# Moving a row norm from GpSimd to ScalarE, with GpSimd left to form its scale and bias

## The chip, the cores and the metric

The kernel runs on one core of one Trainium2 chip. The metric is the time of one execution in device microseconds (us); lower is better. The engines of the core run unsynchronized and meet by semaphores: TensorE (PE, its weight loads PEld), VectorE (DVE), ScalarE (ACT), GpSimd (POOL) and SyncE (SP), which here issues most of the DMAs.

## The reference, cut to what matters

```python
xn = _layernorm(A_q)                    # rows of 448: (x - mean) / sqrt(var + 1e-5)
k_shift = causal depthwise conv of A_k with 4 taps (A_shift_k)
kv = k_shift * A_v
y  = long causal convolution of kv with A_ssm_k (FFT, length 4096) + kv * A_ssm_D
h  = xn @ B_w1 + B_b1                   # 448 -> 1792
out = A_q + xn * y + mish(h) @ B_w2     # 1792 -> 448
```

There are 2048 rows of 448 numbers, all float32. The change is about how `xn` is formed for the dense part (`h`).

## The kernel before, in words

**Two strands, one TensorE.** The dense part (MLP) runs over 8 chunks of 256 rows; each chunk is two tiles `jj` of 128 rows. Within a chunk 7 pairs `p` of 128 hidden columns are worked one after the other. Between them stand, by hand-written slot numbers, the steps of the long convolution: first transforms of the filter and of `kv` (`f1_mm`, `f1_fold`, `f1_out`, slots up to 63), then eight octants of products (`h2_mm`, `v2_mm`, `prod`, `i1_mm`), then the inverse transform and the gate (`i2_mm`, `gate`). The program order on every engine is the order in which the Python code issues; nothing reorders it.

**A pair.** Pair number i has two slots. Slot 2i: `g1_mm(i)`, 22 matmuls into a PSUM tile `pg` (L447), in float32r with high and low halves. Slot 2i+1: `mish(i)`, where ScalarE reads `pg` into `a` (L455, two instructions), then casts `a` to its high half `ach` (L73), and VectorE forms the low half `acl` (L74); and `g2_mm(i-2)`, 12 matmuls that use `ach` and `acl` (L472 to L474). The PSUM tiles `pg` are a ring of two, shared by `g1_mm` and by the transposes of `xn`: `g1_mm(i+2)` waits until `mish(i)` has read its tile. The tiles `pc` of the convolution are another ring of two.

**The norm.** `ln_stats(c)` puts six small steps for chunk c into a list `drip`; `dv()` takes one from it after each VectorE instruction of other work, so that they are spread out. The first five are VectorE's: `stats` of both tiles (L379), `aggr` of both (L382: mean and variance into `mv`), `eps` (L385: variance plus 1e-5 into `ve`). The sixth issues `power` (L388, GpSimd: `ve` to the power -0.5 into `rstd`), `norm` for both tiles (L392: subtract the mean, multiply by `rstd`) and `tail` (L396: a copy of the last 64 columns behind the row). `norm` and `tail` are on GpSimd for chunks 1 to 6, and on VectorE for chunks 0 and 7.

**What uses it.** `ln_T(c, jj)` transposes `xn` on TensorE (L407), ScalarE casts the result to the high half `XH` (L419), and VectorE forms the low half `XL` (L417). For tile 0 this stands in front of `mish` of the last pair but one of the chunk before, for tile 1 in front of `g1_mm` of the last pair.

**Other work on the same queues.** Chunk 0 also splits weights: ScalarE casts `w2h` (L73) and `w1h` (L338), VectorE forms `w2l` (L74) and `w1l` (L343, L345). For the convolution ScalarE copies `st` (L130), `hs` (L209), `vs` (L218) and `qe` (L249) out of `pc`, and issues the stores of `st` and `qe` on its own DMA queue (L139, L250); VectorE folds `st` (L131, L133), works the taps (L153 to L165) and the products (L231).

Of the kernel before, what the change touches and what calls it, by code (L numbers as in the profile page):

```python
# [7 lines left out]
F32 = mybir.dt.float32  # L8
F32R = mybir.dt.float32r
AF = mybir.ActivationFunctionType  # L10
ALU = mybir.AluOpType
# [3 lines left out]
S, D, F = 2048, 448, 1792  # L15
NJ = 16
# [3 lines left out]
NCHUNK = S // CH  # L20
# [16 lines left out]
def tile_kernel(ctx: ExitStack, tc, q, k, v, sk, hT, sD, w1, b1, w2, c_f1, c_g, c_gi, c_i2, out):  # L37
    nc = tc.nc
    V = nc.vector

    def pool(name, bufs=1, stack=ctx, **kw):
        return stack.enter_context(tc.tile_pool(name=name, bufs=bufs, **kw))

    cp = pool("consts")
# [14 lines left out]
    f1id = cp.tile([128, 2, 128], F32, name="f1id")  # L59
    f1, ident = f1id[:, 0], f1id[:, 1]  # L60
    mhalf = cp.tile([128, 2], F32, name="mhalf")
    b1t = cp.tile([128, NF], F32, name="b1t")
    mv = cp.tile([128, NJ, 2], F32, name="mv")
    rstd = cp.tile([128, NJ], F32, name="rstd")
# [190 lines left out]
    EE, QA, Q = {}, {}, {}  # L255
# [115 lines left out]
    def ln_parts(c):  # L371
        st = mp.tile([128, 2, 6], F32, name="bst", bufs=2)
        ve = mp.tile([128, 2], F32, name="ve", bufs=2)
        xn = mp.tile([128, 2, D + 64], F32, name="xn", tag="xn", bufs=1)
        XN[c] = xn
        eng = nc.gpsimd if 0 < c < NCHUNK - 1 else V

        def stats(jj):
            V.bn_stats(st[:, jj], Q[c][:, jj])  # L379

        def aggr(jj):
            V.bn_aggr(mv[:, 2 * c + jj], st[:, jj])  # L382

        def eps(a, b):
            V.tensor_scalar(ve[:, a:b], mv[:, 2 * c + a:2 * c + b, 1], EPS, None, op0=ALU.add)  # L385

        def power(a, b):
            nc.gpsimd.tensor_tensor(rstd[:, 2 * c + a:2 * c + b], ve[:, a:b], mhalf[:, a:b], op=ALU.pow)  # L388

        def norm(jj):  # L390
            j = 2 * c + jj
            eng.tensor_scalar(xn[:, jj, :D], Q[c][:, jj], mv[:, j, 0:1], rstd[:, j:j + 1],  # L392
                              op0=ALU.subtract, op1=ALU.mult)

        def tail(a, b):
            eng.tensor_copy(xn[:, a:b, D:], xn[:, a:b, D - 64:D])  # L396

        return stats, aggr, eps, power, norm, tail

    def ln_stats(c):  # L400
        stats, aggr, eps, power, norm, tail = ln_parts(c)
        drip.extend([lambda: stats(0), lambda: stats(1), lambda: aggr(0), lambda: aggr(1), lambda: eps(0, 2),
                     lambda: [f(*a) for f, *a in ((power, 0, 2), (norm, 0), (norm, 1), (tail, 0, 2))]])
# [169 lines left out]
            at(t + 2 + m, gate_out, c)  # L573

    V.memset(mhalf, -0.5)
    one = cp.tile([128, NJ], F32, name="one")
    V.memset(one, 1.0)
    ve0 = cp.tile([128, 2], F32, name="ve0")
# [12 lines left out]
    nc.sync.dma_start(b1t, b1)  # L591
    h_load(2)
    stats, aggr, eps, power, norm, tail = ln_parts(0)
    for jj in range(2):
        stats(jj)
# [20 lines left out]
    for s in range(nslots):  # L616
        j = s // 2 - G2_LAG - 1
# [70 lines left out]
```

## Time and profile before

| | |
|---|---|
| time, three runs | 382.29, 382.82, 383.46 us; median 382.82 |
| span of the profiled execution | 382.4 us; the page gives no other time for that execution, and the median of the runs is 0.4 us above it |
| TensorE busy | 368.1 us (96%) |
| VectorE busy | 277.9 us (73%) |
| ScalarE busy | 158.8 us (42%) |
| GpSimd busy | 50.5 us (13%) |
| mean granted TensorE clock | 0.983 |

The busy shares are means over stages that differ: VectorE is above 90% in the stage with the taps and around 50% later. In a timeline row the columns are start, duration, engine, line, operation, written tile<-read tiles, size, count; what stands in brackets is the idle time of the engine before the row and what ended it.

### The profile page before, as it was taken

The page shows a single profiled execution, that of the slowest core. Times are in us where ns is not written, and L with a number is a line of the kernel's source. Part 1 is how long each engine was busy: PE and PEld are TensorE (multiplying, and loading weights), DVE is VectorE, ACT ScalarE, POOL GpSimd, SP SyncE. Part 2 cuts the span into 40 slices and gives each one's busy share as a digit, 9 for nine tenths or more (in the row PEclk, how much of TensorE's full clock was granted, in tenths as well). Part 3 has the DMA queues.
Part 4 walks back from the last instruction along what each step waited for, and adds up shares of the span by engine and source line. Part 5 has one row for each costly group of instructions (what it writes and reads, how often), then busy time and mean ns, then how long its engine had stood idle before and what let it go on. Part 6 is the DMA issues. An engine that isn't in the chain of part 4 may idle for free.

```text
span 382.4 us, 7472 instructions
## 1 busy us (share of the span) xinstructions
PE 368.1 (96%) x3126; PEld 295.4 (77%) x3126; DVE 277.9 (73%) x369; ACT 158.8 (42%) x265; POOL 50.5 (13%) x47
## 2 busy tenths in 40 slices
PE   5999999999999999999999999999999999999984
PEld 1888888978888988988876776667666798768954
DVE  2799858999999998997434745843954724989393
ACT  2587543344233433433443755653755334122310
POOL 2006000700042003200023000240000040220000
PEclk8599999999999999999999999999999999999998
DMA  7799986839588427604885687967570759999566
GB/s 266 288 269 339 363 317 173 250 68 300 126 289 213 117 51 249 192 4 96 255 265 175 207 268 245 289 225 241 199 265 2 243 155 233 239 228 254 194 185 248
DMA packets 32851, 82.11 MB, mean 215 GB/s; under 512 B 2993, under 2 KB 18226, under 8 KB 32818
## 3 DMA queue, kind: packets, MB, share of 16 engines
q1 hardware_dynamic: 22498, 52.72, 43.0%
q10 hardware_dynamic: 9200, 22.50, 19.9%
q0 software_dynamic: 1120, 6.42, 7.1%
q8 instruction: 24, 0.39, 0.4%
q14 instruction: 9, 0.07, 0.1%
HBM read 53.19 MB, written 28.44 MB: 213 GB/s over the span
## 4 chain that ended last, share of the span: by engine, by line
PE 60%; DMA 19%; DVE 13%; ACT 3%; issue 3%; POOL 1%; ACTq 0%; SPq 0%; DVEq 0%
PE pg L447 25%; PE pg L472 7%; PE pc L198 7%; PE pg L474 6%; PE pg L473 6%; DMA e<-E 6%; DMA out_dram<-q 5%; PE pc L124 4%; PE pc L241 3%; DMA a<-ACC 3%; PE pg L407 2%; DVE x L162 2%; DMA kr<-in_k_dram 2%; DMA f1id<-in_c_f_dram 1%; DMA Dkv<-st 1%
## 5 line engine op out<-in xcount | busy, mean ns | idle before, releaser
L455 ACT ACTIVATE a<-pg,b1t 128x256 f32<-128x256 f32 x112 | 47.1, 473 | 122.8 <-PE pg L447 104.8
L447 PE MATMUL pg<-XH,w1h 128*128 128x256 f32 x448 | 92.2, 288 | 1.6 <-DVE XL L417 0.9
L447 PEld LDWEIGHTS pg<-XH,w1h 128*128 128x128 f32 x448 | 70.8, 191 | 18.9 <-issue 15.0
L472 PE MATMUL pg<-w2h,ach 128*128 128x448 f32 x224 | 83.2, 371 | 0.2 <-DVE qt L479 0.2
L474 PE MATMUL pg<-w2h,acl 128*128 128x448 f32 x224 | 81.4, 363 | 0.0
L473 PE MATMUL pg<-w2l,ach 128*128 128x448 f32 x224 | 81.3, 363 | 0.0
L74 DVE TENSOR_TENSOR acl<-a,ach 128x512 fp32r<-128x512 f32 x56 | 38.4, 687 | 48.6 <-ACT ach L73 48.4
L447 PE MATMUL pg<-XL,w1h 128*128 128x256 f32 x448 | 70.4, 279 | 0.0
L447 PEld LDWEIGHTS pg<-XL,w1h 128*128 128x128 f32 x448 | 60.3, 190 | 0.0
L447 PE MATMUL pg<-XH,w1l 128*128 128x256 f32 x336 | 57.4, 280 | 0.0
L472 PEld LDWEIGHTS pg<-w2h,ach 128*128 128x128 f32 x224 | 42.0, 187 | 12.7 <-issue 10.4
L447 PEld LDWEIGHTS pg<-XH,w1l 128*128 128x128 f32 x336 | 47.5, 191 | 0.0
L473 PEld LDWEIGHTS pg<-w2l,ach 128*128 128x128 f32 x224 | 42.1, 188 | 2.5 <-DVE w2l L74 0.2
L474 PEld LDWEIGHTS pg<-w2h,acl 128*128 128x128 f32 x224 | 42.1, 188 | 2.5
L388 POOL TENSOR_TENSOR rstd<-ve,mhalf 128x2 f32<-128x2 f32 (+1 forms) x9 | 7.7, 859 | 265.7 <-DVE ve L385 265.7
L73 ACT CAST ach<-a 128x512 fp32r<-128x512 f32 x56 | 34.7, 620 | 1.8
L392 POOL TENSOR_SCALAR xn<-qt,mv,rstd 128x448 f32<-128x448 f32 x12 | 28.4, 2371 | 0.6
L162 DVE TENSOR_TENSOR x<-x 128x896 f32<-128x896 f32 x24 | 27.0, 1123 | 0.8
L419 ACT CAST XH<-pg 128x512 fp32r<-128x512 f32 x16 | 9.4, 588 | 38.3 <-PE pg L407 38.2
L417 DVE TENSOR_TENSOR XL<-pg,XH 128x512 fp32r<-128x512 f32 x16 | 11.0, 688 | 14.4 <-ACT XH L419 14.1
L130 ACT COPY st<-pc 128x896 f32<-128x896 f32 x16 | 14.5, 909 | 15.6 <-PE pc L124 13.3
L124 PE MATMUL pc<-x,f1id 32*64 32x448 f32 x256 | 17.3, 585 | 3.2 <-DMA f1id<-in_c_f_dram 3.2
(62 smaller groups left out, 394.4 us busy)
## 6 DMA issues: line engine op xcount, KB each, us to landing
Dh<-st ACTq DMA_DIRECT2D x16, 448.0 KB, 5.5
Dkv<-st ACTq DMA_DIRECT2D x16, 448.0 KB, 5.2
ah<-Dh SPq DMA_DIRECT2D x8, 896.0 KB, 5.5
av<-Dkv SPq DMA_DIRECT2D x8, 896.0 KB, 4.8
E<-qe ACTq DMA_DIRECT2D x8, 896.0 KB, 4.1
e<-E POOLq DMA_DIRECT2D x14, 448.0 KB, 14.6
kr<-in_k_dram SPq DMA_DIRECT2D x10, 448.0 KB, 7.1
x<-in_hT_dram SPq DMA_DIRECT2D x8, 448.0 KB, 6.5
```

What stands on the lines that cost most here:

```text
L73: nc.scalar.copy(h, raw)
L74: V.tensor_sub(l, raw, h)
L124: nc.tensor.matmul(ps[h][64 * jj:64 * jj + 64, b, :D], f1[rg:rg + 32, 0:64], x[rg:rg + 32, jj], start=True, stop=True, tile_position=(rg, ...
L130: nc.scalar.copy(st[:, 1], o)
L162: V.tensor_add(KV[g], KV[g], o)
L198: nc.tensor.matmul(p[32 * t:32 * t + 32, r, :D], g[rs, t, c], a[rs, t], start=True, stop=True, tile_position=(64 * r, 32 * t))
L392: eng.tensor_scalar(xn[:, jj, :D], Q[c][:, jj], mv[:, j, 0:1], rstd[:, j:j + 1], op0=ALU.subtract, op1=ALU.mult)
L447: nc.tensor.matmul(ps[:, n], l, r, start=n_ == 0, stop=n_ == len(mm) - 1)
L455: nc.scalar.activation(a[:, n], ps[:, n], AF.Mish, bias=b1t[:, 2 * p + n:2 * p + n + 1])
L472: nc.tensor.matmul(ps, ah[:, n, cs], w2h[:, f], start=f == 0, stop=False)
L473: nc.tensor.matmul(ps, ah[:, n, cs], w2l[:, f], start=False, stop=False)
L474: nc.tensor.matmul(ps, al[:, n, cs], w2h[:, f], start=False, stop=f == NF - 1)
```

## The change

For chunks 1 to 7 `xn` is written by one ScalarE instruction per tile, as `rstd * x + shift`, and ScalarE makes the 64-column copy too. GpSimd forms `shift = -mean * rstd`: it multiplies the mean by -1 before `power` and by `rstd` behind it. Chunk 0 keeps VectorE's form. One more small memset stands at the start.

```diff
+    mone = cp.tile([128, 2], F32, name="mone")
+    shift = cp.tile([128, NJ], F32, name="shift")
...
-        eng = nc.gpsimd if 0 < c < NCHUNK - 1 else V
...
         def power(a, b):
-            nc.gpsimd.tensor_tensor(rstd[:, 2 * c + a:2 * c + b], ve[:, a:b], mhalf[:, a:b], op=ALU.pow)
+            r, m = (t[:, 2 * c + a:2 * c + b] for t in (rstd, shift))
+            if c:
+                nc.gpsimd.tensor_tensor(m, mv[:, 2 * c + a:2 * c + b, 0], mone[:, a:b], op=ALU.mult)
+            nc.gpsimd.tensor_tensor(r, ve[:, a:b], mhalf[:, a:b], op=ALU.pow)
+            if c:
+                nc.gpsimd.tensor_tensor(m, m, r, op=ALU.mult)

         def norm(jj):
             j = 2 * c + jj
-            eng.tensor_scalar(xn[:, jj, :D], Q[c][:, jj], mv[:, j, 0:1], rstd[:, j:j + 1],
-                              op0=ALU.subtract, op1=ALU.mult)
+            if c:
+                nc.scalar.activation(xn[:, jj, :D], Q[c][:, jj], AF.Identity, bias=shift[:, j:j + 1],
+                                     scale=rstd[:, j:j + 1])
+            else:
+                V.tensor_scalar(xn[:, jj, :D], Q[c][:, jj], mv[:, j, 0:1], rstd[:, j:j + 1],
+                                op0=ALU.subtract, op1=ALU.mult)

         def tail(a, b):
-            eng.tensor_copy(xn[:, a:b, D:], xn[:, a:b, D - 64:D])
+            (nc.scalar.copy if c else V.tensor_copy)(xn[:, a:b, D:], xn[:, a:b, D - 64:D])
...
     V.memset(mhalf, -0.5)
+    V.memset(mone, -1.0)
```

The orders on TensorE and SyncE are the same in both kernels; VectorE's differs by the memset and by the norm of chunk 7. In the rows below the source lines of the changed kernel are 2 to 11 higher than those before.

GpSimd, from the start to the norm of chunk 1. Before:

```order
L343 TENSOR_TENSOR w1l<-kr,w1h 128x3x128
L388 TENSOR_TENSOR rstd<-ve,mhalf 128x2
L392 TENSOR_SCALAR xn<-qt,mv,rstd 128x448 x2
L396 COPY xn<-xn 128x2x64
L388 TENSOR_TENSOR rstd<-ve,mhalf 128x2
```

And now:

```order
L345 TENSOR_TENSOR w1l<-kr,w1h 128x3x128
L391 TENSOR_TENSOR shift<-mv,mone 128x2
L392 TENSOR_TENSOR rstd<-ve,mhalf 128x2
L394 TENSOR_TENSOR shift<-shift,rstd 128x2
L391 TENSOR_TENSOR shift<-mv,mone 128x2
```

The large passes are gone, and two two-column products stand around each power.

ScalarE in chunk 0, where the norm of chunk 1 is issued, between the weight casts of one pair and the `mish` of the next (`a` is what `mish` writes, `Dh<-st` a store that ScalarE issues). Before:

```order
L73 CAST ach<-a 128x512
L73 CAST w2h<-kr 128x896
L338 CAST w1h<-kr 128x4x256
L139 DMA Dh<-st 64x2x896 x2
L455 ACTIVATE a<-pg_337,b1t 128x256 x2
L73 CAST ach<-a 128x512
L73 CAST w2h<-kr 128x896
L338 CAST w1h<-kr 128x4x256
L130 COPY st<-pc 128x896
L455 ACTIVATE a<-pg_404,b1t 128x256 x2
```

And now:

```order
L75 CAST ach<-a 128x512
L75 CAST w2h<-kr 128x896
L340 CAST w1h<-kr 128x4x256
L399 ACTIVATE xn<-qt,shift,rstd 128x448 x2
L406 COPY xn<-xn 128x2x64
L141 DMA Dh<-st 64x2x896 x2
L465 ACTIVATE a<-pg_342,b1t 128x256 x2
L75 CAST ach<-a 128x512
L75 CAST w2h<-kr 128x896
L340 CAST w1h<-kr 128x4x256
L132 COPY st<-pc 128x896
L465 ACTIVATE a<-pg_409,b1t 128x256 x2
```

The norm and its copy stand in front of the two stores and of the next `mish`.

ScalarE in chunk 5, among the octants, where the norm of chunk 6 is issued. Before:

```order
L455 ACTIVATE a<-pg_2624,b1t 128x256 x2
L73 CAST ach<-a 128x512
L249 COPY qe<-pc 128x896 x2
L250 DMA E<-qe 128x4x448
L209 COPY hs<-pc 128x896 x2
L455 ACTIVATE a<-pg_2726,b1t 128x256 x2
L73 CAST ach<-a 128x512
L218 COPY vs<-pc 128x896 x2
```

And now:

```order
L465 ACTIVATE a<-pg_2637,b1t 128x256 x2
L75 CAST ach<-a 128x512
L251 COPY qe<-pc 128x896 x2
L252 DMA E<-qe 128x4x448
L399 ACTIVATE xn<-qt,shift,rstd 128x448 x2
L406 COPY xn<-xn 128x2x64
L211 COPY hs<-pc 128x896 x2
L465 ACTIVATE a<-pg_2739,b1t 128x256 x2
L75 CAST ach<-a 128x512
L220 COPY vs<-pc 128x896 x2
```

The norm stands in front of the two copies `hs`, which empty the two `pc` tiles.

## The prediction

> **What bounds the kernel now.** I read the page's first part, then the waits, then ScalarE, VectorE and TensorE around each of the seven norms in the timeline.
>
> ```profile
> PE 368.1 (96%) x3126; PEld 295.4 (77%) x3126; DVE 277.9 (73%) x369; ACT 158.8 (42%) x265; POOL 50.5 (13%) x47
> ACT a L455 <- PE pg L447: 104.8, 42, 6.8
> DVE acl L74 <- ACT ach L73: 48.4, 23, 6.1
> ```
>
> TensorE is busy 96% of 382.4 us, so the end moves only if TensorE has to wait more or less. ScalarE is 42% busy and spends 104.8 us waiting for TensorE: it has room for more work. But these are sums. VectorE waits 48.4 us for `ach`, so what holds ScalarE up at the wrong moment holds VectorE, and through `XL` or a PSUM tile TensorE. The question is at which moment ScalarE meets each norm.
>
> **What the change takes away and adds.** GpSimd loses 12 passes of 2.37 us and the short copies behind them. They run beside other work, and no TensorE instruction waits for their end. What goes with them is their effect on VectorE: of the sums L162 below, which are alike, the first ran beside GpSimd.
>
> ```profile
> L392 POOL TENSOR_SCALAR xn<-qt,mv,rstd 128x448 f32<-128x448 f32 x12 | 28.4, 2371 | 0.6
> 70.53 1.41 DVE L162 TENSOR_TENSOR x<-x 128x896 f32<-128x896 f32 x1
> 83.15 1.09 DVE L162 TENSOR_TENSOR x<-x 128x896 f32<-128x896 f32 x1
> L338 ACT CAST w1h<-kr 128x1024 fp32r<-128x1024 f32 x6 | 6.3, 1044 | 0.3 <-DMA kr<-in_w_dram 0.3
> L73 ACT CAST ach<-a 128x512 fp32r<-128x512 f32 x56 | 34.7, 620 | 1.8
> 155.38 0.29 POOL L396 COPY xn<-xn 128x128 f32<-128x128 f32 x1
> ```
>
> ScalarE gains per chunk two norms and a copy. From the two casts a ScalarE pass costs 0.20 us and 0.83 ns per column: 0.57 us for 448 columns. For scale and bias read per row I add 0.1 each (0 to 0.2): 0.76; two of them overlap a little, 1.4 together. The copy of 128 columns is 0.3, behind a wait for the norms. That is 1.75 us per chunk and 12 us in all, against 104.8 us of idling: its length is not the trouble.
>
> GpSimd gains two products of 128x2 per chunk. The one behind the power is on the path. No row shows such a product. Near it are the fastest copy of 128 columns (0.29 us) and the 128x2 powers, in the rows below 0.71 to 1.48. I take 0.3, as for the short copy, since nothing in it is a power; the ends are 0 and 1.48. With a hop of 0.1 us on each side (below, `ve` ends at 31.85 and GpSimd starts at 31.93), ScalarE can start the norm 0.5 us after the power ends.
>
> The memset at the start (one more of two columns on VectorE) costs nothing, since TensorE's first long wait is ended by a DMA (the row of 8.08, further down). That VectorE loses the norm of chunk 7 I cost at nothing too, since ScalarE does it at the same time (below).
>
> **Where ScalarE meets the norm.** The norm is queued at the place where the sixth step of the list is issued in program order. ScalarE gets there when its own earlier work is done, not when VectorE has computed `ve`. Before, only idle GpSimd waited for `ve`; now ScalarE does, with everything behind the norm in its queue. The Trainium skill says in "TensorE: Matmul & The Clock Gate", section "Architectural detail: the array is 16× 32×32, not 1× 128×128", that ScalarE and VectorE take their queues strictly first in, first out, so nothing passes a waiting norm; by that rule the sum below stands, and if ScalarE could pass over it the sum would be near nothing.
>
> *Norm of chunk 1.* ScalarE, GpSimd, VectorE, TensorE:
>
> ```profile
> 26.95 1.05 ACT L338 CAST w1h<-kr 128x1024 fp32r<-128x1024 f32 x1 [0.33 <-DMA kr<-in_w_dram]
> 27.36 1.24 ACTq L139 DMA_DIRECT2D Dh<-st  x2
> 28.95 0.84 ACT L455 ACTIVATE a<-pg,b1t 128x256 f32<-128x256 f32 x2 [0.95 <-DVE w2l L74]
> 31.93 1.08 POOL L388 TENSOR_TENSOR rstd<-ve,mhalf 128x2 f32<-128x2 f32 x1 [21.51 <-DVE ve L385]
> 31.68 0.17 DVE L385 TENSOR_SCALAR ve<-mv 128x2 f32<-128x2 f32 x1
> 31.76 0.69 DVE L74 TENSOR_TENSOR acl<-a,ach 128x512 fp32r<-128x512 f32 x1
> 35.13 1.09 DVE L131 TENSOR_TENSOR st<-pc,st 128x896 f32<-128x896 f32 x1
> 41.12 0.69 DVE L417 TENSOR_TENSOR XL<-pg,XH 128x512 fp32r<-128x512 f32 x1
> 44.16 0.60 PE L447 MATMUL pg<-XH,w1h 128*128 128x256 f32 x3
> ```
>
> ScalarE is through with the `w1h` cast at 28.0 and now waits for GpSimd: the first product delays the power to 32.1, which ends at 33.2; the second ends at 33.6, the norms run 33.7 to 35.1, the copy to 35.45. The two stores queued next take 1.24 us to issue, so `mish` starts at 36.8 instead of 28.95. `ach` ends at 38.3 and `acl` starts at 38.35 instead of 31.76. VectorE then waits for `w2h` (0.94 us, to 39.15) and `w1h` (to 40.1), which stand behind `ach` in ScalarE's queue: the fold L131 starts at 41.6 instead of 35.13. From there it had 6.0 us to `XL` without idling: `XL` starts at 47.6 and ends at 48.3. The last `g1_mm` of chunk 0 takes its PSUM tile from that `XL`, and starts at 48.35 instead of 44.16: **+4.2**. (2.35 us of the delay fall into slack.)
>
> *Norm of chunk 2.* ScalarE is idle from 67.25 to `mish` at 68.99, and meets the norm there:
>
> ```profile
> 68.53 0.72 POOL L388 TENSOR_TENSOR rstd<-ve,mhalf 128x2 f32<-128x2 f32 x1 [29.43 <-DVE ve L385]
> 68.99 0.84 ACT L455 ACTIVATE a<-pg,b1t 128x256 f32<-128x256 f32 x2 [1.74 <-PE pg L447]
> 71.86 0.68 DVE L74 TENSOR_TENSOR acl<-a,ach 128x512 fp32r<-128x512 f32 x1
> 84.90 0.62 PE L447 MATMUL pg<-XH,w1h 128*128 128x256 f32 x3 [0.55 <-DVE XL L417]
> ```
>
> The norm starts at 69.75, the copy ends at 71.5, `mish` runs at 71.55 instead of 68.99, and `acl` starts at 73.1 instead of 71.86. VectorE has no idle from there to the `XL` for which TensorE waits at 84.90. 0.35 us come back, since two later instructions no longer run beside GpSimd. **+0.9**.
>
> *Norm of chunk 3.* The `st` copy is queued behind the norm:
>
> ```profile
> 108.78 0.91 ACT L130 COPY st<-pc 128x896 f32<-128x896 f32 x1 [2.36 <-PE pc L124]
> 110.61 1.01 POOL L388 TENSOR_TENSOR rstd<-ve,mhalf 128x2 f32<-128x2 f32 x1 [34.36 <-DVE ve L385]
> 112.09 1.08 DVE L131 TENSOR_TENSOR st<-pc,st 128x896 f32<-128x896 f32 x1
> 124.42 0.68 DVE L417 TENSOR_TENSOR XL<-pg,XH 128x512 fp32r<-128x512 f32 x1
> 125.35 0.60 PE L447 MATMUL pg<-XH,w1h 128*128 128x256 f32 x3
> ```
>
> The norm runs 112.1 to 113.5, the copy ends at 113.85, `st` is copied by 114.75, the fold L131 starts at 114.8 instead of 112.09. 0.35 come back beside the missing GpSimd work; `XL` ends at 127.45, and `g1_mm` starts then instead of at 125.35: **+2.1**.
>
> *Norm of chunk 4.* ScalarE idles from 145.5 on, up to a `mish` that now stands behind the norm:
>
> ```profile
> 149.33 0.84 ACT L455 ACTIVATE a<-pg,b1t 128x256 f32<-128x256 f32 x2 [3.82 <-PE pg L447]
> 149.60 0.71 POOL L388 TENSOR_TENSOR rstd<-ve,mhalf 128x2 f32<-128x2 f32 x1 [32.76 <-DVE ve L385]
> 151.99 0.68 DVE L74 TENSOR_TENSOR acl<-a,ach 128x512 fp32r<-128x512 f32 x1
> 163.94 0.62 PE L447 MATMUL pg<-XH,w1h 128*128 128x256 f32 x3 [0.39 <-DVE XL L417]
> ```
>
> The norm starts at 150.8, the copy ends at 152.55, `mish` runs at 152.6 instead of 149.33, `ach` ends at 154.1, and `acl` starts then instead of at 151.99. 0.2 come back, and TensorE already waits for `XL` at 163.94: **+1.9**.
>
> *Norms of chunks 5 and 7*: behind the place ScalarE idles 6.3 us and 3.9 us, and 1.75 us fit; the power of chunk 5 ends at 198.7, 6.4 us ahead of the row. Nothing.
>
> ```profile
> 198.01 0.71 POOL L388 TENSOR_TENSOR rstd<-ve,mhalf 128x2 f32<-128x2 f32 x1 [42.34 <-DVE ve L385]
> 205.14 0.59 ACT L419 CAST XH<-pg 128x512 fp32r<-128x512 f32 x1 [6.30 <-PE pg L407]
> 316.78 0.59 ACT L419 CAST XH<-pg 128x512 fp32r<-128x512 f32 x1 [3.86 <-PE pg L407]
> ```
>
> *Norm of chunk 6.* Here ScalarE reaches it at 242.3, and the `hs` copies stand behind it:
>
> ```profile
> 244.18 1.72 ACT L209 COPY hs<-pc 128x896 f32<-128x896 f32 x2 [1.87 <-PE pc L198]
> 246.53 1.48 POOL L388 TENSOR_TENSOR rstd<-ve,mhalf 128x2 f32<-128x2 f32 x1 [42.51 <-DVE ve L385]
> 247.47 1.73 PE L198 MATMUL pc<-av,g 64*32 64x448 f32 x32
> ```
>
> The power ends at 248.0, the norms run 248.5 to 249.9, the copy to 250.25, the first `hs` copy to 251.15. `v2_mm` needs both `pc` tiles that `hs` empties, and starts at 251.2 instead of 247.47: **+3.7**, straight on TensorE.
>
> **The sum.** 4.2 + 0.9 + 2.1 + 1.9 + 0 + 3.7 + 0 = 12.8. The span goes from 382.4 to 395.2 us; the median of the runs stands 0.4 above the span. Some later wait of TensorE for a DMA may go: I forecast 395 us. All delays were worked out at the places of before; I let them add, since VectorE waits for `ach` 23 times over the span, and so is mostly back in step with TensorE before the next norm.
>
> **The rivals.**
>
> *Only part arrives.* If VectorE makes good its lateness in chunks 2 to 4 (it is 73% busy on the whole), only the two large terms stay: 4.2 + 3.7, 390 us. Against it: at 84.90 and 163.94 TensorE already waits for VectorE.
>
> *The two products are slow.* If each takes as long as the five powers above on the mean (1.0 us), the wait grows by 0.7 us at five places, and in chunk 1 twice: +4.2, 399 us. At the slowest power's 1.48 it would be 402; at 0, 393.
>
> *The clock falls.* At the start TensorE idled 3.17 us before 8.08, and the granted clock (third column from the end, in windows of 4 us) stood at a half until about 17.7:
>
> ```profile
> 8.08 1.80 PE L124 MATMUL pc<-x,f1id 32*64 32x448 f32 x16 [3.17 <-DMA f1id<-in_c_f_dram]
> 8.00:12.00 4.00, 3.83 (x24) 1.80 (x24) 2.97 (x8) 1.05 (x3) 1.72 (x2) 0.50 1.04 404
> 16.00:20.00 4.00, 4.00 (x30) 4.00 (x29) 2.44 (x3) 2.29 (x4) 0.00 (x0) 0.79 0.89 341
> ```
>
> The wait of 3.7 us in chunk 6 could do the same: some 10 us at half speed lose 5, 400 us. The page "TensorE: Matmul & The Clock Gate" of the Trainium skill (Part 1) has the clock fall after an idle window of some 3.4 us that runs freely, which a gap of 3.7 would fill only by luck.
>
> *Faster, by freeing VectorE.* If ScalarE's waits fell into its own idle time, what remained would be VectorE beside no GpSimd work: 0.35 us in chunk 2, 0.35 in chunk 3, 0.2 in chunk 4, where VectorE bounds TensorE, so 381.5 us. The Trainium skill's "Advanced Engine Details and Errata" says that GpSimd shares an SBUF interface with VectorE and conflicts with its two-input instructions; the pair L162 agrees (1.41 against 1.09). It decides only from the point where `ve` is ready before ScalarE arrives; in chunk 6 it is 4 us behind (242.3 against 246.5), in chunks 1 to 4 by 1 us or more.
>
> *No change*: the delays end in slack everywhere, within 0.3% (1.15 us, about what a measurement here can tell from no change).
>
> **How the numbers follow.** Forecast, 391 to 398 us: 0.52. Part arrives, 385 to 391: 0.17. Slow products or a fallen clock, above 398: 0.20 (half each). Faster: 0.07. No change: 0.04. So slower has 0.89. A range from 387.5, a little below the second case's 390, to 401, which holds the third's 399 and 400, leaves out under 2 in 10.
>
> **What would show it.** Right: ScalarE's norm rows have idle ahead of them that GpSimd's second product ends, some 6 us in chunks 1 and 6; TensorE waits for `XL` at the last `g1_mm` of chunk 0 and for `hs` at `v2_mm` near 260. Wrong: those waits of TensorE are missing, or the products take a microsecond, or the norm takes much over 0.76 us.

## The result, and the profile after

| | before | after |
|---|---|---|
| median of 4 runs each | 383.14 us (382.29 to 383.95) | 400.24 us (399.70 to 401.13) |
| ratio | 1 | 1.0448, 95% interval 1.0420 to 1.0477 |
| span of the profiled execution | 382.4 us | 398.1 us, in a run of 399.89 us |

The change costs 17.1 us; 12 to 13 were forecast. The 400.24 us lie inside the range, but above 398, in the band that the prediction held at 0.20. A run takes 1.8 us more than its span, not the 0.4 that the prediction put on it from two different executions.

The head of the page after, and from its waits the rows of ScalarE's new wait and of the TensorE and VectorE waits that have grown (total, times, longest):

```profile
PE 371.4 (93%) x3126; PEld 295.7 (74%) x3126; DVE 274.8 (69%) x367; ACT 169.9 (43%) x286; POOL 24.3 (6%) x43
ACT xn L399 <- POOL shift L394: 26.0, 6, 6.3
DVE acl L76 <- ACT ach L75: 61.5, 24, 6.1
PE pc L200 <- ACT hs L211: 4.2, 2, 3.7
PE pg L457 <- DVE XL L427: 3.1, 2, 2.7
PE pg L482 <- ACT w2h L75: 3.0, 1, 3.0
PE pc L126 <- DVE x L167: 2.7, 2, 2.0
```

ScalarE stands still 26.0 us in front of six of the seven norms, until GpSimd's second product is done. It is only one point busier than before (43% against 42%), so the shares of the page do not show the loss. VectorE's wait for `ach` grew from 48.4 to 61.5 us.

The new instructions, minimum, median and maximum in ns:

```profile
L399 ACT ACTIVATE xn<-qt,shift,rstd x14: 746/754/767, 32.0 to 329.2; 128x448 f32<-128x448 f32 x14
L406 ACT COPY xn<-xn x7: 297/298/301, 33.4 to 329.9; 128x128 f32<-128x128 f32 x7
L391 POOL TENSOR_TENSOR shift<-mv,mone x7: 195/197/948, 30.8 to 319.2; 128x2 f32<-128x2 f32 x7
L394 POOL TENSOR_TENSOR shift<-shift,rstd x7: 194/426/1027, 31.8 to 325.3; 128x2 f32<-128x2 f32 x7
```

The norm (0.754 us, forecast 0.76) and the copy (0.298, forecast 0.3) came out as estimated. The second product is 0.43 us at the median, and anything from 0.19 to 1.03.

**Where the time went.** TensorE runs the same matmuls in the same order in both kernels, so each can be paired with itself. The lag of the changed kernel at a few of them, with the jump since the row above:

| matmul, start before -> after, us | lag | jump |
|---|---|---|
| L473, 24.03 -> 22.85 | -1.2 | the clock came up earlier at the start of this execution |
| `g2_mm` of the third pair, 34.95 -> 37.10 | 2.2 | +3.3, norm of chunk 1 |
| the next `g1_mm`, 37.35 -> 42.50 | 5.2 | +3.0: 0.9 of waiting for `w2l`, then slow matmuls |
| `f1_mm`, 76.25 -> 82.22 | 6.0 | +0.8, norm of chunk 2 |
| `f1_mm`, 121.15 -> 129.15 | 8.0 | +2.0, norm of chunk 3 |
| `g1_mm`, 163.94 -> 174.45 | 10.5 | +2.5, norm of chunk 4 |
| `v2_mm`, 247.47 -> 261.59 | 14.1 | +3.6, norm of chunk 6 |
| the `g2_mm` behind it, 249.14 -> 264.76 | 15.6 | +1.5, `v2_mm` was slow |

The jumps add to 16.7 us, near the 17.1 measured; the 1.2 us at the start are luck of this one execution. Nothing is lost at the norms of chunks 5 and 7. The five places in the timeline after, first the norm of chunk 1:

```profile
26.74 1.05 ACT L340 CAST w1h<-kr 128x1024 fp32r<-128x1024 f32 x1 [1.08 <-DMA kr<-in_w_dram]
31.98 1.42 ACT L399 ACTIVATE xn<-qt,shift,rstd 128x448 f32<-128x448 f32 x2 [4.19 <-POOL shift L394]
33.43 1.24 ACTq L141 DMA_DIRECT2D Dh<-st  x2
34.72 0.84 ACT L465 ACTIVATE a<-pg,b1t 128x256 f32<-128x256 f32 x2 [0.99 <-PE pg L457]
36.12 0.93 ACT L75 CAST w2h<-kr 128x896 fp32r<-128x896 f32 x1
37.10 0.74 PE L482 MATMUL pg<-w2h,ach 128*128 128x448 f32 x1 [2.95 <-ACT w2h L75]
38.23 0.74 PE L483 MATMUL pg<-w2l,ach 128*128 128x448 f32 x1 [0.39 <-DVE w2l L76]
```

ScalarE waits 4.19 us, norms, issues the two stores, and `mish` comes right behind their issue, at 34.72. (The bracket of that row names `pg`, but the matmuls that this `mish` reads had ended at 27.85: nothing passed the waiting norm.) TensorE does not get as far as `XL`: `g2_mm` needs the cast `w2h`, two instructions behind `mish`, and waits 2.95 us for it. The second matmul follows the first by 1.13 us instead of 0.20, since `w2l` is late too, and the matmuls of 128x448 take 0.57 to 0.74 us instead of 0.36. Chunks 2, 3 and 4 (for each ScalarE's wait, VectorE's, TensorE's):

```profile
74.89 1.42 ACT L399 ACTIVATE xn<-qt,shift,rstd 128x448 f32<-128x448 f32 x2 [2.29 <-POOL shift L394]
78.06 0.69 DVE L76 TENSOR_TENSOR acl<-a,ach 128x512 fp32r<-128x512 f32 x1 [1.09 <-ACT ach L75]
82.22 1.01 PE L126 MATMUL pc<-x,f1id 32*64 32x448 f32 x16 [0.61 <-DVE x L167]
118.15 1.42 ACT L399 ACTIVATE xn<-qt,shift,rstd 128x448 f32<-128x448 f32 x2 [5.86 <-POOL shift L394]
120.74 1.09 DVE L133 TENSOR_TENSOR st<-pc,st 128x896 f32<-128x896 f32 x1 [2.67 <-ACT st L132]
129.15 1.01 PE L126 MATMUL pc<-x,f1id 32*64 32x448 f32 x16 [2.04 <-DVE x L167]
159.57 1.41 ACT L399 ACTIVATE xn<-qt,shift,rstd 128x448 f32<-128x448 f32 x2 [5.92 <-POOL shift L394]
162.74 0.69 DVE L76 TENSOR_TENSOR acl<-a,ach 128x512 fp32r<-128x512 f32 x1 [3.25 <-ACT ach L75]
174.45 0.62 PE L457 MATMUL pg<-XH,w1h 128*128 128x256 f32 x3 [2.67 <-DVE XL L427]
```

Each time the wait goes from ScalarE to VectorE and, with VectorE busy all the way, some 4 to 12 us later to TensorE. For the norm of chunk 6 there is no VectorE between:

```profile
258.99 1.41 ACT L399 ACTIVATE xn<-qt,shift,rstd 128x448 f32<-128x448 f32 x2 [6.34 <-POOL shift L394]
260.64 1.71 ACT L211 COPY hs<-pc 128x896 f32<-128x896 f32 x2
261.59 3.24 PE L200 MATMUL pc<-av,g 64*32 64x448 f32 x32 [3.71 <-ACT hs L211]
```

The two slow stretches, in windows of 4 us (third column from the end: the granted clock):

```profile
36.00:40.00 4.00, 2.51 (x6) 1.88 (x7) 3.55 (x5) 3.97 (x7) 0.00 (x0) 0.52 0.80 190
40.00:44.00 4.00, 4.00 (x19) 3.70 (x18) 3.97 (x5) 1.98 (x3) 0.00 (x0) 0.63 0.92 292
260.00:264.00 4.00, 2.41 (x32) 0.62 (x32) 0.23 (x1) 3.94 (x8) 0.00 (x0) 0.68 0.06 16
264.00:268.00 4.00, 4.00 (x44) 2.60 (x36) 0.46 (x1) 1.45 (x2) 0.00 (x0) 0.90 0.44 125
```

Behind both of its long waits TensorE's clock stood at a half for a while. Behind the waits of 0.61, 2.04 and 2.67 us in chunks 2 to 4 it stayed at 1.00.

### The profile page after: what moved, and what is told of

Its sections match the earlier page's. It is cut to its first block, busy times and chain, and to the rows that moved or that the text cites. A ratio compares the mean times of both kernels' runs of the same rounds, so it can differ in the third digit from the quotient of the medians.

```text
span 398.1 us, 7484 instructions
## 1 busy us (share of the span) xinstructions
PE 371.4 (93%) x3126; PEld 295.7 (74%) x3126; DVE 274.8 (69%) x367; ACT 169.9 (43%) x286; POOL 24.3 (6%) x43
## 4 chain that ended last, share of the span: by engine, by line
PE 43%; DVE 22%; DMA 18%; ACT 8%; issue 4%; POOL 2%; ACTq 1%; DVEq 0%; SPq 0%; POOLq 0%
PE pg L457 16%; PE pc L200 7%; DMA e<-E 5%; PE pg L482 5%; DMA out_dram<-q 5%; PE pg L483 5%; PE pg L484 5%; DVE x L164 3%; DMA a<-ACC 2%; PE pc L243 2%; DMA Dkv<-st 2%; DVE acl L76 2%; DVE st L133 2%; PE pc L126 2%; ACT a L465 2%
## 5 line engine op out<-in xcount | busy, mean ns | idle before, releaser
L482 PE MATMUL pg<-w2h,ach 128*128 128x448 f32 x224 | 84.4, 377 | 3.1 <-ACT w2h L75 3.0
L483 PE MATMUL pg<-w2l,ach 128*128 128x448 f32 x224 | 82.4, 368 | 1.0 <-DVE w2l L76 1.0
L484 PE MATMUL pg<-w2h,acl 128*128 128x448 f32 x224 | 82.3, 367 | 0.0
L76 DVE TENSOR_TENSOR acl<-a,ach 128x512 fp32r<-128x512 f32 x56 | 38.3, 686 | 61.7 <-ACT ach L75 61.5
L457 PE MATMUL pg<-XL,w1h 128*128 128x256 f32 x448 | 69.6, 277 | 0.0
L457 PEld LDWEIGHTS pg<-XL,w1h 128*128 128x128 f32 x448 | 59.4, 188 | 0.0
L164 DVE TENSOR_TENSOR x<-x 128x896 f32<-128x896 f32 x24 | 26.2, 1090 | 0.8
L126 PE MATMUL pc<-x,f1id 32*64 32x448 f32 x256 | 17.1, 576 | 5.5 <-DMA f1id<-in_c_f_dram 2.9
L133 DVE TENSOR_TENSOR st<-pc,st 128x896 f32<-128x896 f32 x16 | 17.4, 1088 | 6.1 <-ACT st L132 5.7
L399 ACT ACTIVATE xn<-qt,shift,rstd 128x448 f32<-128x448 f32 x14 | 9.9, 755 | 26.0 <-POOL shift L394 26.0
L391 POOL TENSOR_TENSOR shift<-mv,mone 128x2 f32<-128x2 f32 x7 | 2.8, 395 | 287.4 <-DVE mv L383 287.4
```

The costliest lines, as they stand in the source:

```text
L76: V.tensor_sub(l, raw, h)
L126: nc.tensor.matmul(ps[h][64 * jj:64 * jj + 64, b, :D], f1[rg:rg + 32, 0:64], x[rg:rg + 32, jj], start=True, stop=True, tile_position=(rg, ...
L133: V.tensor_add(st[:, 0], e, st[:, 1])
L164: V.tensor_add(KV[g], KV[g], o)
L457: nc.tensor.matmul(ps[:, n], l, r, start=n_ == 0, stop=n_ == len(mm) - 1)
L482: nc.tensor.matmul(ps, ah[:, n, cs], w2h[:, f], start=f == 0, stop=False)
```

## The experiments

The theory: it is the wait in ScalarE's in-order queue, at five of seven places, that costs the time. The rivals: the length of ScalarE's added work by itself; GpSimd's products by themselves; a cost per moved norm that is alike everywhere. Each ratio is against runs of the kernel before on the same chip, with its 95% interval.

**The wait without the work.** GpSimd keeps the norm; ScalarE only reads `rstd` at the place of the norm.

```diff
+    def look(c):
+        nc.scalar.copy(mp.tile([128, 2], F32, name="lk", bufs=2), rstd[:, 2 * c:2 * c + 2])
...
-                     lambda: [f(*a) for f, *a in ((power, 0, 2), (norm, 0), (norm, 1), (tail, 0, 2))]])
+                     lambda: [f(*a) for f, *a in ((power, 0, 2), (look, c), (norm, 0), (norm, 1), (tail, 0, 2))]])
```

> The kernel before, with one 128x2 ScalarE copy of rstd put at the place in ScalarE's queue where the changed kernel has the norm; GpSimd still makes the norm. The wait without the work. Theory (ScalarE meets the norm before the power is there, and everything behind it waits): the wait ends some 0.4 us sooner than in the changed kernel, and 1.75 us less work stands behind it. Chunk 1: mish at about 34.5 instead of 28.95, w2h about 2 us late for g2_mm: +2 to 3. Chunk 2: 0. Chunk 3: the st copy ends at 112.8, +0.75. Chunk 4: +0.1. Chunk 6: v2_mm at 249.3 instead of 247.5, +1.8. Together +5, 388 us, up to 391 if the clock falls in chunk 1. Rival (the length of ScalarE's added work costs the time): about 383 us.

Measured: 387.83 us (386.14 to 391.42), 1.0135 (1.0084 to 1.0185), +5. A read of two columns, 0.19 us long, costs 5 us where it stands:

```profile
ACT lk L401 <- POOL rstd L388: 23.3, 6, 5.7
PE pc L198 <- ACT hs L209: 2.0, 2, 1.5
PE pg L475 <- ACT w2h L73: 1.2, 1, 1.2
251.56 0.19 ACT L401 COPY lk<-rstd 128x2 f32<-128x2 f32 x1 [5.73 <-POOL rstd L388]
251.66 1.71 ACT L209 COPY hs<-pc 128x896 f32<-128x896 f32 x2
```

ScalarE waits nearly as long as in the changed kernel (23.3 against 26.0 us), but what stands behind is released some 2 us sooner: in chunk 6 `hs` starts 0.10 us behind the read, and 1.65 us behind the start of the norm in the changed kernel, whose second product adds some 0.6 more. So less of it reaches TensorE.

**The work without the wait.** Two passes of the norm's size and the copy at the five places, on operands that are ready; `xn` is then overwritten by GpSimd's norm.

```diff
+    def work(c):
+        if c in (5, 7):
+            return
+        d = XN[c]
+        for jj in range(2):
+            nc.scalar.activation(d[:, jj, :D], Q[c][:, jj], AF.Identity, bias=mhalf[:, 0:1], scale=mhalf[:, 1:2])
+        nc.scalar.copy(d[:, :, D:], d[:, :, D - 64:D])
...
-                     lambda: [f(*a) for f, *a in ((power, 0, 2), (norm, 0), (norm, 1), (tail, 0, 2))]])
+                     lambda: [f(*a) for f, *a in ((power, 0, 2), (work, c), (norm, 0), (norm, 1), (tail, 0, 2))]])
```

> The kernel before, with two ScalarE passes of 128x448 (scale and bias from a constant tile) and the 128-column copy put into ScalarE's queue at the places of the norms of chunks 1, 2, 3, 4 and 6; they write xn, which GpSimd then overwrites with the true norm. The work without the wait, since the operands are there long before. Theory: ScalarE idles at all five places when it gets there, so 0 to +1 us, 383 to 384. Rival (length of the work): 5 times 1.75, up to +9, 392 us.

Measured: 383.08 us, 1.0000 (0.9981 to 1.0019).

```profile
L405 ACT ACTIVATE xn<-qt,mhalf 128x448 f32<-128x448 f32 x10 | 7.1, 754 | 0.5 <-ACT qe L249 0.5
```

The same ten passes of 754 ns, with 0.5 us of idling in front of them instead of some 25, cost nothing. So the length of the work by itself is out. Behind a wait it is not: the wait alone costs 5 us, the work alone nothing, both together, with GpSimd's products in the chain, 17, since each of the five places is then released some 2 us later, and the clock falls more.

**The norm issued later.** GpSimd's steps stay; ScalarE's norm waits in a list until the fifth or sixth pair.

```diff
-                     lambda: [f(*a) for f, *a in ((power, 0, 2), (norm, 0), (norm, 1), (tail, 0, 2))]])
+                     lambda: (power(0, 2), held.append((norm, tail)))])
...
+    def norm_now():
+        for norm, tail in held:
+            norm(0)
+            norm(1)
+            tail(0, 2)
+        held.clear()
...
+                    if p >= NP - 3:
+                        norm_now()
```

> The changed kernel, with the two norms and the copy issued later: GpSimd's power and products stay where they are, ScalarE's norm stands in front of g1_mm of the fifth pair of a chunk or, where the power has not been issued by then (chunks 5 and 7), of the sixth. The work stays on ScalarE, the wait goes, since the power is done when ScalarE gets there. Theory: no loss at any of the five places, and VectorE keeps the 0.9 us that it gains without GpSimd's passes beside it: 382 to 384 us, against 383 before. Rival (ScalarE's added work, or GpSimd's small products by themselves): 390 us or more.

Measured: 381.60 us, 0.9959 (0.9943 to 0.9975): a little faster than both kernels, and than the 382 to 384 us expected. It has the same products on GpSimd and the same work on ScalarE as the changed kernel, so neither costs the time by itself.

```profile
L399 ACT ACTIVATE xn<-qt,shift,rstd 128x448 f32<-128x448 f32 x14 | 9.9, 754 | 2.1 <-POOL shift L394 2.1
L162 DVE TENSOR_TENSOR x<-x 128x896 f32<-128x896 f32 x24 | 27.0, 1123 | 0.8
L164 DVE TENSOR_TENSOR x<-x 128x896 f32<-128x896 f32 x24 | 26.2, 1091 | 0.8
```

The first row is of this kernel: 2.1 us of waiting are left. The second is VectorE's sum of the taps before, the third the same sum here: 32 ns less on the mean, where no GpSimd pass runs beside it.

**Which norms.** ScalarE takes the norm only for the chunks in a tuple, (5, 7) here and (1,), (6,) and (2, 3, 4) in the next three; the others stay as in the kernel before.

```diff
+ACT_NORM = (5, 7)
...
+        act = c in ACT_NORM
+        eng = nc.gpsimd if 0 < c < NCHUNK - 1 else V
...
-            if c:
+            if act:
```

> ScalarE makes the norm of chunks 5 and 7 alone; chunks 1 to 4 and 6 stay on GpSimd as before. Theory: both places lose nothing, since ScalarE idles behind them: 383 us (382 to 384.5). Rival (each moved norm costs about the same): 2 of 7 times 17, +5, 388 us.

> ScalarE makes the norm of chunk 1 alone, all others as before. Theory, revised by the trace of the changed kernel (g2_mm of the third pair waits for the w2h cast that stands behind the norm, and the clock falls in that wait): +3 for the wait and up to +3 for the clock, 386 to 390 us, against 383. By the step of the prediction (XL for the last g1_mm of chunk 0): +4.2, 387. Rival (all norms cost alike): 17 by 7, +2.5, 385.5.

> ScalarE makes the norm of chunk 6 alone. Theory: v2_mm waits for hs, +3.7, and +1.5 more where the clock falls in that wait: 386.5 to 388.5 us. Rival (all alike): 385.5.

> ScalarE makes the norms of chunks 2, 3 and 4. Theory: 0.8 + 2.0 + 2.5 as in the trace of the changed kernel, +5.3, 388.5 us (387 to 389.5), with no fall of the clock, since TensorE's waits stay at 2.5 us and below. With the two runs of chunk 1 and 6 the three losses add to the 17 us of the change if they are independent. Rival (VectorE makes its lateness good when it has met no earlier delay): 384.

| ScalarE's norms | time, us | ratio (interval) |
|---|---|---|
| 5 and 7 | 382.41 | 0.9968 (0.9942 to 0.9994) |
| 1 | 388.83 | 1.0166 (1.0133 to 1.0199) |
| 6 | 388.25 | 1.0155 (1.0119 to 1.0192) |
| 2, 3 and 4 | 387.01 | 1.0127 (1.0095 to 1.0160) |

The losses of the last three rows add to 4.48%, with 0.6 either way by their intervals, and with the first row's gain to 4.16%; the whole change is 4.48%. So within the error they are independent, and nothing is made good between them. A norm does not cost the same everywhere: 6.3 and 5.9 us for chunks 1 and 6, 1.6 on the mean for 2 to 4, none for 5 and 7.

**TensorE kept busy in its two long waits.** Matmuls with zero weights, added into a PSUM tile that is being summed: four in front of `g2_mm` of the third pair, five in front of `v2_mm` of the fifth octant.

```diff
+    def fill(n, key):
+        for _ in range(n):
+            nc.tensor.matmul(P2[key][0:32, :D], zero, one[:, 0:1].to_broadcast([128, D]), start=False, stop=False)
...
+        if o == 4:
+            fill(5, (5, 0))
...
+                if j == 2:
+                    fill(4, (0, 0))
```

> The changed kernel, with TensorE given work that changes no result (matmuls with zero weights, added into a PSUM tile that is being summed) in the two longest waits: four in front of g2_mm of the third pair, five in front of v2_mm of the fifth octant. Theory of the clock (it falls because TensorE idles 3 us and more): the clock stays up, g2_mm and v2_mm run at full rate, 4 to 5 us of the loss come back less what the fill is longer than the wait: 395 to 397 us instead of 400. Rival (the slow matmuls behind the waits have another cause, such as w2l late on VectorE): 400 us or more.

Measured: 394.20 us, 1.0318 (1.0287 to 1.0350), against 1.0448 without the fill: 1.3%, 5.0 us back (3.4 to 6.6 by the two intervals).

```profile
34.30 3.21 PE L215 MATMUL pg<-one,zero 128*32 128x448 f32 x8
38.44 0.47 PE L489 MATMUL pg<-w2l,ach 128*128 128x448 f32 x1 [0.53 <-DVE w2l L76]
257.48 3.96 PE L215 MATMUL pg<-one,zero 128*32 128x448 f32 x10
261.38 1.74 PE L200 MATMUL pc<-av,g 64*32 64x448 f32 x32
36.00:40.00 4.00, 3.47 (x13) 1.88 (x12) 3.34 (x5) 3.97 (x7) 0.00 (x0) 1.00 0.80 189
ACT xn L405 <- POOL shift L400: 26.4, 6, 6.3
```

ScalarE waits as long as before (26.4 us), but the clock stays at 1.00 at both places and `v2_mm` takes 1.74 us instead of 3.24. The second matmul of `g2_mm` still comes 1.00 us behind the first (37.44), so that part of the loss is the wait for `w2l` and not the clock. That leaves 2.1 us at `g2_mm` and 1.5 at `v2_mm`, 3.6 in the trace; with the 5.0 of the runs, some 4 to 5 of the 17 us were the clock, not waiting. (In this trace the clock fell once more, in chunk 4; see the last section.)

**Two more products on GpSimd's chain.**

```diff
+                for _ in range(2):
+                    nc.gpsimd.tensor_tensor(m, m, one[:, a:b], op=ALU.mult)
```

> The changed kernel, with two more 128x2 products by one on GpSimd behind the one that ends the chain. In the changed kernel such a product took 0.20 to 1.03 us, 0.45 on the mean, so each adds some 0.5 us with its hop, and the norm comes 1.0 us later. Theory (at five places ScalarE waits for this chain, and its wait passes to TensorE one to one): 5 times 1.0, +5, 405 us (403 to 408). Rival (the delay of ScalarE is partly hidden, so that its size doesn't count): 400 to 401 us.

Measured: 406.00 us, 1.0607 (1.0572 to 1.0643), 1.6% or 6 us above the changed kernel. ScalarE's wait grew from 26.0 to 31.7 us, 1.4 of it at chunk 5, where nothing is lost:

```profile
ACT xn L401 <- POOL shift L396: 31.7, 6, 6.9
84.00:88.00 4.00, 2.06 (x17) 0.69 (x18) 3.97 (x6) 0.17 (x1) 0.00 (x0) 0.70 0.86 260
180.00:184.00 4.00, 3.45 (x18) 3.45 (x19) 3.97 (x7) 0.00 (x0) 0.00 (x0) 0.64 0.00 0
```

A longer chain is passed on to TensorE, but the 6 us are not waiting alone. TensorE's waits at the five places are longer by 4.1 us together, 2.2 of them in chunk 2, and the clock also fell behind the waits of chunks 2, 3 and 4 (0.70 and 0.64 in the windows shown, 0.67 from 132 to 136), where it stood at 1.00 in the trace of the changed kernel. That the delay counts is shown; that each us of it costs one us is not.

**Late, without chunks 5 and 7.** The late kernel, with the norms of chunks 5 and 7 made as before.

```diff
+ACT_NORM = (1, 2, 3, 4, 6)
```

> The kernel with the late norm, but with the norms of chunks 5 and 7 made as before (GpSimd, VectorE). It tells where the 0.4% of the late kernel come from. If from GpSimd's passes beside VectorE in the stage with the taps (chunks 2 to 4): the gain stays about half or more, 0.2 to 0.3%, 382 against 383. If from chunks 5 and 7 alone: no gain.

Measured: 381.04 us, 0.9962 (0.9942 to 0.9982). The gain stays whole, so it does not need chunks 5 and 7. That the relief of VectorE is its cause agrees with the row of L164, but was not tried by itself. Why chunks 5 and 7 alone came out a little below 1 too is open; their interval reaches to 0.9994.

## Why the prediction came out as it did

The mechanism was right: ScalarE meets the norm before GpSimd is done, everything behind it in its queue is late, and five places pay while two do not. The wait without the work, the work without the wait and the late norm each showed it. The main case of 391 to 398 us did not come, though: the sum of 12.8 us had no term for the clock.

Step by step, with the lags of the table above:

- *Chunk 1, +4.2 forecast, +3.3 and then +3.0.* The size of the first part was near by luck, for its path was wrong. The sum followed `acl` and the fold to the `XL` of the last `g1_mm` and left out that the cast `w2h`, which it did time (39.15), feeds TensorE directly through `g2_mm` of the third pair. That wait comes first, `w2l` is 0.9 us late behind it, and the clock falls. The wait of TensorE for `XL` at the last `g1_mm` of chunk 0, one of the signs that were to show the prediction right, is missing. ScalarE's wait was 4.19 us, not some 6: the norm came 1.7 us earlier than worked out (31.98 against 33.7), since the power took 0.70 us, not 1.08, and the execution was ahead.
- *Chunk 2, +0.9 forecast, +0.8.* VectorE waited 1.09 us for `ach` (1.24 worked out).
- *Chunk 3, +2.1 forecast, +2.0.* The size held, the place did not: TensorE waited not for `XL` but, one step earlier, for the tap sum L167 in front of `f1_mm`; so it did in chunk 2.
- *Chunk 4, +1.9 forecast, +2.5.* The second product took 1.03 us here, not 0.3.
- *Chunk 6, +3.7 forecast, +3.6 and then +1.5.* `v2_mm` waited 3.71 us for `hs`, as worked out; the rest is the clock.
- *The clock, a rival at half of 0.20.* It fell at both long waits. This is the term that the sum lacked: 2.1 + 1.5 us in the trace, 5.0 by the fill, where the rival had 5 us for chunk 6 alone. It was weighed for one place only, and taken to need luck.
- *Only part arrives* was wrong: the separate losses add to the whole within the error. *Slow products* was right in direction (0.43 at the median for 0.3), and once they took the microsecond that was named as a sign of being wrong.
- *Faster, by freeing VectorE* had the right size of gain, 0.9 us and more, once the wait is taken away: 1.5 us in the late kernel.

That the estimates let the delays add was right, and the runs with some of the norms show it.

## What to carry to other kernels

Before an instruction is moved to another engine's queue, look up the time at which that engine reaches the place, and the time at which the operands are there; where the operands come later, the difference and the instruction's own length delay all that stands behind it; the engine's busy share does not show this. Here the length alone cost nothing, the wait alone 5 us and both together 17. While only GpSimd, which had nothing else to do, waited for the late operand, it cost nothing; issuing ScalarE's norm later, when its operands were ready, turned the loss into a gain of 0.4%. Follow every instruction behind the wait to TensorE, the nearest first, and allow for a half-speed clock behind a wait of a few us (2.1 and 1.5 us at the two falls in the changed kernel).

## What the runs showed of the hardware that was not expected

The clock fell after waits well under the 3.2 us from which the prediction took it, and not after every longer one. In the kernel with the wait alone TensorE idled 1.23 and 0.66 us within one stretch of 3.4 us and was busy 1.60 of it; the next stretch ran at a half:

```profile
33.40:36.80 3.40, 1.60 (x12) 1.12 (x10) 1.75 (x3) 3.37 (x6) 3.33 (x3) 1.00 0.91 237
36.80:40.20 3.40, 3.31 (x9) 2.96 (x10) 3.30 (x5) 3.37 (x6) 0.18 (x1) 0.50 0.69 185
```

The idle window of some 3.4 us that the Trainium skill gives ("TensorE: Matmul & The Clock Gate", Part 1), taken as a window without any work, is thus too long a condition here: less was enough. The length of a wait does not decide by itself either. Chunk 4 in the kernel with the fill and in the changed kernel, then the start of the kernel with the norms of chunks 2 to 4 alone:

```profile
172.55 0.62 PE L463 MATMUL pg<-XH,w1h 128*128 128x256 f32 x3 [2.58 <-DVE XL L433]
172.00:176.00 4.00, 3.45 (x19) 3.45 (x20) 3.97 (x7) 0.00 (x0) 0.00 (x0) 0.67 0.00 0
172.00:176.00 4.00, 1.55 (x13) 1.55 (x14) 3.97 (x6) 0.41 (x1) 0.00 (x0) 1.00 0.21 61
9.13 1.80 PE L127 MATMUL pc<-x,f1id 32*64 32x448 f32 x16 [3.49 <-DMA f1id<-in_c_f_dram]
8.00:12.00 4.00, 2.87 (x22) 1.50 (x23) 2.95 (x7) 0.62 (x1) 1.72 (x2) 1.00 1.03 401
```

After 2.58 us the clock fell; after 2.67 us in the changed kernel (the row of 174.45) and after 3.49 us it stayed at 1.00, where 3.17 us at the start of the kernel before were followed by a half. What decides was not tried.

GpSimd's product of two columns took between 0.19 and 1.03 us, a factor of five. Of the three fast second products two (31.75 and 325.33) stand where VectorE idles, the third (74.65) does not; what sets their time was not tried.
